# The last of eighteen groups takes the seven-product form of its first matmul; VectorE adds partial sums out of PSUM and scales the group ahead of it

## Chip, core and metric

The kernel runs on one core of a Trainium2 chip. The metric is device time in microseconds (us) of one launch; the time before is the median of nine runs. The engines are TensorE (PE in the profile; PEld is its weight load), VectorE (DVE), ScalarE (ACT), GpSimd (POOL, which here does small arithmetic and starts accumulating DMAs) and SyncE (SP, which starts plain DMAs).

## The reference

The input `x` is (8, 4224, 192) in float32. A causal convolution over the sequence with seven taps comes first, one softmax-normed set of taps for each of eight heads; then a layer norm without an offset, two matmuls with a ReLU between them, and a residual.

```python
w = softmax(weight, axis=-1)                       # (8 heads, 7 taps)
x_unf = x_pad[:, idx, :].reshape(B, S, K, H, group)
x = np.einsum('hk,bskhg->bshg', w, x_unf).reshape(B, S, D)
xn = (x - mu) / np.sqrt(var + 1e-06) * g_ln
ch = np.maximum(xn @ w_ch1, 0.0) @ w_ch2           # 192 -> 768 -> 192
out = x + ch
```

All of it is float32. The kernel folds `g_ln` and the subtraction of the mean into the first weight, so the norm is left as one factor for each row, which is applied to the result of the second matmul (`scale`, with `rstd`).

## The kernel before

**Tiling.** A row of `x` is one position of the sequence. Each of 128 partitions holds a run of neighbouring rows, and a group is up to `J` = 16 rows on every partition. There are 18 groups: three small ones (0 to 2, with 6, 8 and 10 rows), and fifteen of 16 rows (3 to 17). For a group, VectorE and ScalarE compute the convolution into `y`, VectorE transposes it in blocks of 32x32 into `yt` (j rows, `NC` = 6 chunks of 32 channels, 32 columns), TensorE forms the hidden layer (the "up" stage), ScalarE moves it from PSUM into `room` with the ReLU, and TensorE forms the output (the "down" stage). `room` is one buffer; each group uses it anew.

**Matmuls.** In the up stage `rows_of_tiles` issues matmuls of 32 contracted rows; four of them, on four row strips (`NQ` = 4), run together and fill four PSUM banks. One matmul of the program is two MATMUL records of the trace, as float32 goes in two passes. The eight PSUM banks are used as two sets of four (`take_set`).

**Seven products.** Groups in `MIXED` (3 to 16 before) run `up_mixed`. There the `yt` of the group is cut in two by rows and in two by channels (`quarters_of_y`), and the first weight in two by channels and in two by hidden units; two thirds of the hidden units (`PAIR` = 2 of `FC` = 3 chunks in each half) are formed by seven products of quarter size instead of eight (Strassen's scheme in Winograd's form, with sums of quarters made by VectorE in `sums_of_y`), and the remaining chunks by two full products (`plain`). Partial results stay in PSUM from one product to the next (the set called `chain`), and three others are added to a result that already lies in `room`: ScalarE copies the partial sum from PSUM into a spare room (`first`, `second`, `third`), and `close` has GpSimd start a DMA that adds it. Both sets alternate, so a product can begin only when the set's earlier content was read. `up_mixed` also holds, in the order in which they are written, the ScalarE multiplications that scale the output of the group ahead (`scale(g - 1, ...)`), its store (`add_to_out`, a DMA from GpSimd that adds to the output in DRAM) and the next group's taps on VectorE (`conv`).

**Down stage.** `down_fast` forms the output for `fast[g]` rows with seven products again; here VectorE forms the sums (`half_sum`) in `room` itself. For groups 3 to 16 `fast[g]` is all 16 rows. For the last group, 17, `fast` is 11; the other 5 rows go through `down`, plain matmuls, after `down_fast`, so that the end of the kernel has little left after the last matmul.

**The last group before.** Group 17 isn't in `MIXED`. It runs `up`: for each of 6 chunks of hidden units, one product over 11 rows (352 columns) and one over 5 rows (160 columns); ScalarE evicts them, with four instructions for the 11 rows (L519) and one for the 5 (L521). `lower_sum(17)` makes its three sums on VectorE afterwards. Group 16 is scaled by ScalarE between the evictions of the first chunks (16 instructions on L830), and its two stores follow on GpSimd.

The order of instructions on every engine is the order in which the program is written (`manual_schedule`); the framework adds the semaphores.

Of the kernel before, what the change touches and what calls it, by code (L numbers as in the profile page):

```python
# [10 lines left out]
AF = mybir.ActivationFunctionType  # L11
ALU = mybir.AluOpType
# [4 lines left out]
def kernel(  # L17
# [36 lines left out]
    C = 32  # L54
# [25 lines left out]

    MIXED = range(3, NG - 1)
    PAIR = NF // 2 - 1
# [397 lines left out]

    def blocks(g):

        n = groups[g][2]
        cut = fast[g] if 0 < fast[g] < n else n // 2 if n * C > 512 else 0
        return [slice(0, cut), slice(cut, n)] if cut else [slice(0, n)]

    def hidden_tile(g):
        n = groups[g][2]

        cut = NF * NQ * fast[g] * C  # L490
        halves = rest = None
        if fast[g]:
            halves = room[:, 0:cut].rearrange(
                "p (h e f q j t) -> p h e f q j t", h=2, e=2, f=FC, q=NQ, t=width(g)
            )
        if n > fast[g]:
            rest = room[:, cut : NF * NQ * n * C].rearrange(
                "p (f q j t) -> p f q j t", f=NF, q=NQ, t=C
            )
        ht[g] = halves, rest  # L500

    def width(g):

        return T if fast[g] % 2 or fast[g] < groups[g][2] else C

    def evict_up(g, f, js, src):

        halves, rest = ht[g]
        if js.stop > fast[g]:
            dst = rest[:, f, :, js.start - fast[g] : js.stop - fast[g]]  # L510
            src = src.rearrange("p q (j t) -> p q j t", t=C)
        elif width(g) == C:
            dst = halves[:, :, f // FC, f % FC].rearrange("p h q j t -> p q h (j t)")
            src = src.rearrange("p q (h w) -> p q h w", h=2)
        else:
            dst = halves[:, :, f // FC, f % FC, :, js].rearrange("p h q j t -> p q j h t")
            src = src.rearrange("p q (j h t) -> p q j h t", h=2, t=T)
            for q in range(NQ):
                nc.scalar.activation(dst[:, q], src[:, q], AF.Relu)  # L519
            return  # L520
        nc.scalar.activation(dst, src, AF.Relu)  # L521

    def rows_of_tiles(banks, left, right, first=True, last=True):


        chunks, w = right.shape[2] // P, left.shape[1] * C
        for c in range(left.shape[2]):
            for i in range(chunks):
                for q in range(NQ):
                    rows = slice(C * q, C * q + C)  # L530
                    nc.tensor.matmul(  # L531
                        banks[:, q, i * w : i * w + w], right[rows, c, P * i : P * i + P],
                        left[rows, :, c, :], start=(first and c == 0 and i == 0),
                        stop=(last and c == left.shape[2] - 1), skip_group_check=chunks > 1,
                    )

    def up(g):


        scaled = {0: (), 1: (), 2: (0, 1)}.get(g, (g - 1,))  # L540
        hidden_tile(g)
        for f in range(NF):
            for js in blocks(g):
                banks = take_set()
                rows_of_tiles(banks, yt[g][:, js], w1[:, :, f * P : f * P + P])
                evict_up(g, f, js, banks[:, :, 0 : (js.stop - js.start) * C])
            if g == 0 and f < 2:
                first_tap(1, heads=(H // 2 * f, H // 2 * (f + 1)))

            parts = 2 if g + 1 == NG else 4  # L550
            if 1 <= f <= parts:
                for s in scaled:
                    m = groups[s][2]
                    scale(s, m * (f - 1) // parts, m * f // parts)
                    if f % (parts // 2) == 0:
                        add_to_out(s, m * (f - parts // 2) // parts, m * f // parts)

# [15 lines left out]
    def quarters_of_y(g):  # L573
        return [
            yt[g][:, HJ * h : HJ * h + HJ, CH * k : CH * k + CH] for h in range(2) for k in range(2)
        ]

    def sums_of_y(g):

        room = upool.tile([P, 3 * HJ * CH * C], F32, tag="ys", name=f"ysums{g}")  # L580
        room = room.rearrange("p (v j c t) -> p v j c t", v=3, c=CH, t=C)
        ysums[g] = s1, s2, s3 = [room[:, v] for v in range(3)]
# [11 lines left out]
    def up_mixed(g, last_sum):  # L594


        W = HJ * C
        assert groups[g][2] == fast[g] == 2 * HJ and PAIR * W == 512
        hidden_tile(g)
        a = ht[g][0]  # L600
        a11, a12, a21, a22 = quarters_of_y(g)
# [15 lines left out]

        def close(c, part):
            whole = "p f q w -> p (f q w)"
            add_by_dma(c.rearrange(whole), part.rearrange(whole))  # L620

        def plain(f, banks):
            rows_of_tiles(banks, yt[g][:, 0 : 2 * HJ], w1[:, :, f * P : f * P + P])
            evict_up(g, f, slice(0, 2 * HJ), banks)

# [4 lines left out]
        rooms = parts(bpool, "tb"), parts(cpool, "cs")  # L630
        first, second = (r[:, 0:PAIR] for r in rooms)
        rows_of_tiles(chain, a11, b11, True, False)
        evict(chain, c11)
        rows_of_tiles(other, a12, b21)
        evict(other, first)
        close(c11, first)
        rows_of_tiles(chain, s2, w1sums[:, 1], False, False)
        evict(chain, c21)
        scale(g - 1, 0, 1)
        conv(g + 1, 2, 3)  # L640
        next(last_sum)
        rows_of_tiles(other, s3, w1sums[:, 2], True, False)
        evict(other, c22)
        scale(g - 1, 1, 2)
        rows_of_tiles(chain, s1, w1sums[:, 0], False, False)
        evict(chain, second)
        close(c22, second)
        scale(g - 1, 2, 3)
        rows_of_tiles(other, a22, w1sums[:, 3], False)
        for i, room in enumerate(rooms):  # L650
            one, third = slice(i, i + 1), room[:, PAIR : PAIR + 1]
            evict(other, third, i=one)
            close(c21[:, one], third)
        scale(g - 1, 3, 4)
        rows_of_tiles(chain, s2, b22, False)
        evict(chain, c12, True)
        nc.scalar.activation(c11, c11, AF.Relu)
        scale(g - 1, 4, 7)
        conv(g + 1, 3, 6)
        conv(g + 1, 6, K, heads=(0, H // 2))  # L660
        plain(PAIR, other)
        nc.scalar.activation(c22, c22, AF.Relu)
        scale(g - 1, 7, 10)
        add_to_out(g - 1, 0, 8)
        lower_sum(g, (PAIR,))
        lower_sum(g, range(PAIR))
        conv(g + 1, 6, K, heads=(H // 2, H))
        plain(PAIR + FC, chain)
        scale(g - 1, 10, done)
        add_to_out(g - 1, 8, done)  # L670

    po = {}

    def down(g):


        n = groups[g][2]
        t = ht[g][1]
        po[g] = []
        order = [(c, js) for c in range(NC) for js in blocks(g)]  # L680
        if g + 1 == NG:
            order = [(c, slice(fast[g], n)) for c in range(NC)]
        for c, js in order:
            w = (js.stop - js.start) * C
            bank = take_bank()
            for f in range(NF):
                for q in range(NQ):
                    nc.tensor.matmul(  # L688
                        bank[C * q : C * q + C, 0:w], w2[:, f, C * c : C * c + C],
                        t[:, f, q, js.start - fast[g] : js.stop - fast[g], :],  # L690
                        start=(f == 0), stop=(f == NF - 1),
                    )
            po[g].append((c, js, bank[:, 0:w]))
# [7 lines left out]


    def half_sum(g, dst, left, right, op, fs=range(FC)):
        a = ht[g][0]
        for f in fs:
# [4 lines left out]
    def lower_sum(g, fs=range(FC)):  # L710

        a = ht[g][0]
        if g in MIXED:
# [8 lines left out]
    def down_fast(g):  # L722
        n = fast[g]
        t = width(g)
        w = n * T
        a = ht[g][0]
        flat = cpool.tile([P, NC, NFAST * C], F32, tag="cs", name=f"cs{g}")[:, :, 0 : n * C]
# [35 lines left out]

        taps_behind = [0] * 6
        if g in MIXED:
            taps_behind = [1, 4, 4, 7, 0, 0]
        product(0, a[:, 0, 0], b[0], c11, True)
# [6 lines left out]
        some_taps(taps_behind[3])  # L774
        if g in MIXED:
            transpose(g + 1)
            moments(g + 1, 0, EARLY)
# [9 lines left out]
        if g + 1 == NG:  # L787
            finish_fast(g, 0, flat, cs, parts)
        if g in MIXED:
            close_by_dma(c21, parts[0])  # L790
# [7 lines left out]
    def finish_fast(g, half, flat, cs, parts):  # L798
        n = fast[g]
        ot = ots[g] if half else out_tile(g)  # L800
        if half or g not in MIXED:
            fresh = cs[:, CH * half : CH * half + CH, 1]
# [90 lines left out]
    for g in range(NG):  # L893
# [7 lines left out]
        if not fast[g]:  # L901
# [26 lines left out]
            continue  # L928
        if last:
            lower_sum(g)  # L930
        if g + 2 < NG:
# [49 lines left out]
```

## Time and profile before

| | |
|---|---|
| median of nine runs | 977.62 us (975.88 to 978.59) |
| the profiled execution | 977.75 us, its span 976.1 us |
| TensorE busy | 960.9 us, 98% of the span, granted clock 0.998 |
| VectorE busy | 857.0 us, 88% |
| ScalarE busy | 643.3 us, 66% |
| GpSimd busy | 199.1 us, 20% |
| the last three stages of TensorE: up of group 17, its `down_fast`, its `down` | 31.60, 18.93 and 9.78 us |

The span is the time between the first and the last recorded event of the execution; what lies around it is 1.65 us here. Times inside the profile are counted from the span's start. A row of a group of instructions has line, engine, operation, output and inputs, shapes, count, then busy time and the mean of one in ns, then idle time ahead of it and who ended that. The chain that ended last is followed back from the last instruction.

### The profile page before, as it was taken

What the parts mean: (1) busy time and instruction counts of PE and PEld (TensorE: products, weight loads), DVE (VectorE), ACT (ScalarE), POOL (GpSimd) and SP (SyncE); (2) the same over time, 40 slices, a digit from 0 to 9 for tenths busy, and PEclk for the clock granted to TensorE, in tenths of its full rate; (3) what the DMA queues carried; (4) which work ended last, traced back from release to release, by engine and by line L of the source; (5) the groups of instructions that cost most, each with busy time, mean ns of one, the idle gap of its engine ahead of it and who ended that gap; (6) DMA issues with size and microseconds to landing.
All of it is one profiled execution on the core that took longest, in us unless ns stands there. A gap on an engine that the chain in (4) does not pass through costs nothing.

```text
span 976.1 us, 36329 instructions
## 1 busy us (share of the span) xinstructions
PE 960.9 (98%) x16338; PEld 675.9 (69%) x16338; DVE 857.0 (88%) x1479; ACT 643.3 (66%) x1044; POOL 199.1 (20%) x355
## 2 busy tenths in 40 slices
PE   5999999999999999999999999999999999999997
PEld 4886585766768585776858576675857667685787
DVE  5899998898998989899898989899798989989407
ACT  4733757585867858595776858587685858675451
POOL 2004410411114011411114111321104111230200
PEclk9999999999999999999999999999999999999999
DMA  8333689588696968779686978969697887765131
GB/s 185 110 124 132 143 203 255 114 146 257 135 263 126 238 147 162 227 150 271 128 245 126 201 193 151 265 131 252 132 225 169 145 245 139 186 122 94 23 64 67
DMA packets 29962, 163.19 MB, mean 167 GB/s; under 512 B 3567, under 2 KB 9839, under 8 KB 22126
## 3 DMA queue, kind: packets, MB, share of 16 engines
q0 software_dynamic: 22704, 97.53, 53.3%
q1 hardware_dynamic: 6798, 63.34, 17.0%
q8 instruction: 128, 2.10, 0.9%
q14 instruction: 28, 0.23, 0.1%
q10 hardware_dynamic: 304, 0.00, 0.0%
HBM read 38.95 MB, written 50.33 MB: 91 GB/s over the span
## 4 chain that ended last, share of the span: by engine, by line
PE 97%; DMA 2%; DVE 0%; issue 0%; SPq 0%
PE ps L531 49%; PE ps L741 41%; PE ps L688 6%; DMA xg<-in_x_dram 1%; PE ps L320 1%; DMA ga<-in_moe_g_ln_dram 1%; PE ps L332 0%; PE ps L344 0%; PE ps L349 0%; DVE y L844 0%; DVE ot L869 0%; SPq L165 0%; DVE ot L854 0%; DVE y L857 0%
## 5 line engine op out<-in xcount | busy, mean ns | idle before, releaser
L408 DVE SCALAR_TENSOR_TENSOR y<-xg,taps,y 128x384 f32<-128x384 f32 (+3 forms) x734 | 367.9, 576 | 1.8 <-ACT y L383 1.7
L531 PE MATMUL ps<-yt,w 32*128 32x256 f32 (+5 forms) x4128 | 303.5, 446 | 0.0
L531 PEld LDWEIGHTS ps<-yt,w 32*128 32x128 f32 x4128 | 205.1, 185 | 90.5 <-issue 75.0
L741 PE MATMUL ps<-room,w2sums 128*32 128x256 f32 (+1 forms) x4320 | 233.8, 375 | 0.0
L741 PEld LDWEIGHTS ps<-room,w2sums 128*32 128x32 f32 x4320 | 140.4, 110 | 87.9
L706 DVE TENSOR_TENSOR room<-room 128x1024 f32<-128x1024 f32 (+1 forms) x138 | 154.1, 1188 | 35.6 <-ACT part L747 24.2
L741 PE MATMUL ps<-room,w 128*32 128x256 f32 (+1 forms) x3240 | 179.8, 375 | 0.0
L741 PEld LDWEIGHTS ps<-room,w 128*32 128x32 f32 x3240 | 103.8, 110 | 74.3 <-ACT ot L830 10.6
L747 ACT COPY cs<-ps 128x256 f32<-128x256 f32 (+1 forms) x180 | 63.0, 365 | 99.5 <-PE ps L741 98.8
L531 PE MATMUL ps<-ysums,w1sums 32*128 32x256 f32 x2016 | 111.3, 374 | 0.0
L616 ACT COPY room<-ps 128x2048 f32<-128x2048 f32 x42 | 78.4, 1867 | 48.7 <-PE ps L531 47.4
L531 PEld LDWEIGHTS ps<-ysums,w1sums 32*128 32x128 f32 x2016 | 103.7, 185 | 5.1
L805 DVE STREAM_TRANSPOSE ot<-cs 128x512 f32<-128x512 f32 (+1 forms) x90 | 55.9, 672 | 57.5 <-DMA cs<-part 34.4
L521 ACT ACTIVATE room<-ps 128x2048 f32<-128x2048 f32 (+4 forms) x52 | 75.5, 1451 | 35.7 <-PE ps L531 35.6
L830 ACT ACTIVATE ot<-ot,r 128x192 f32<-128x192 f32 x248 | 96.7, 447 | 0.0
L383 ACT ACTIVATE y<-xg,taps 128x384 f32<-128x384 f32 (+3 forms) x141 | 73.3, 590 | 9.3 <-DMA out_dram<-y 6.9
L837 POOL DMA_DIRECT2D out_dram<-ot x40 | 34.2, 1081 | 207.8 <-ACT ot L830 153.0
L439 DVE BATCH_NORM_STATS2 st<-y 128x6 f32<-128x192 f32 x264 | 71.0, 342 | 0.0
L397 POOL DMA_DIRECT2D y<-tb x28 | 24.6, 1037 | 176.2 <-ACT cs L747 172.8
L394 ACT ACTIVATE tb<-xg,taps 128x384 f32<-128x384 f32 x112 | 58.0, 602 | 0.0
L419 DVE STREAM_TRANSPOSE yt<-y 128x3072 f32<-128x3072 f32 (+3 forms) x19 | 56.2, 2958 | 1.9
L688 PE MATMUL ps<-room,w 128*32 128x192 f32 (+3 forms) x1152 | 57.2, 359 | 0.0
(101 smaller groups left out, 758.7 us busy)
## 6 DMA issues: line engine op xcount, KB each, us to landing
xg<-in_x_dram SPq DMA_DIRECT2D x15, 2112.0 KB, 15.1
out_dram<-ot POOLq DMA_DIRECT2D x29, 768.0 KB, 8.0
y<-tb POOLq DMA_DIRECT2D x28, 768.0 KB, 9.2
out_dram<-y SPq DMA_DIRECT2D x13, 1536.0 KB, 10.7
room<-parts_tb POOLq DMA_DIRECT2D x14, 1024.0 KB, 7.4
room<-parts_cs POOLq DMA_DIRECT2D x14, 1024.0 KB, 7.2
room<-parts_tb POOLq DMA_DIRECT2D x14, 512.0 KB, 9.3
room<-parts_cs POOLq DMA_DIRECT2D x14, 512.0 KB, 10.8
```

The lines of the kernel that those rows point to most:

```text
L383: nc.scalar.mul(y[g][:, 0:n, cs], xg[g][:, 0:n, cs], taps[:, h, 0:1])
L394: nc.scalar.mul(tb[g][:, 0:n, cs], xg[g][:, 1 : 1 + n, cs], taps[:, h, 1:2])
L408: nc.vector.scalar_tensor_tensor(out=y[g][:, 0:n, cs], in0=t[:, k : k + n, cs], scalar=taps[:, h, k : k + 1], in1=y[g][:, 0:n, cs], op0=AL ...
L439: nc.vector.bn_stats(out=sums[g][:, j, :], in_=y[g][:, j, :])
L521: nc.scalar.activation(dst, src, AF.Relu)
L531: nc.tensor.matmul(banks[:, q, i * w : i * w + w], right[rows, c, P * i : P * i + P], left[rows, :, c, :], start=(first and c == 0 and i = ...
L616: nc.scalar.activation(dst, src, AF.Relu) if relu else nc.scalar.copy(dst, src)
L688: nc.tensor.matmul(bank[C * q : C * q + C, 0:w], w2[:, f, C * c : C * c + C], t[:, f, q, js.start - fast[g] : js.stop - fast[g], :], start ...
L706: nc.vector.tensor_tensor(a[:, *dst, f], a[:, *left, f], a[:, *right, f], op=op)
L741: nc.tensor.matmul(dst[C * q : C * q + C, 0:w], right[:, f, C * c : C * c + C], left[:, f, q], start=(first and f == 0), stop=(f == FC - 1 ...
L747: nc.scalar.copy(to[:, c], dst[:, 0:w].rearrange("p (j t) -> p j t", t=t))
L830: nc.scalar.mul(ots[g][:, j, :], ots[g][:, j, :], rstd[g][:, j : j + 1])
```

## The change

Group 17 joins `MIXED` and runs `up_mixed`, then `down_fast` and `down` as before. Five things follow from this.

- Its 16 rows all take part in the seven products. Because `down_fast` of this group works on 11 of the 16 rows, the half-and-half cut isn't made between rows: `quarters_of_y` cuts each block of 32 columns into two of `T` = 16. `room` has one layout for all 16 rows (`h e f q j t`, t = 16), and `of_products` is the view of the first 11.
- In this group, `close` is one VectorE addition that reads the partial sum in PSUM and adds it into `room`, with no copy by ScalarE and no DMA.
- The scaling of group 16 is done by two VectorE multiplications over 8 rows each, put behind the second product's sum; its two stores follow them.
- `sums_of_y(17)` is made by VectorE in the down stage of group 16, ahead of `finish_fast(16)`, as for other groups. `lower_sum` is the form with the ReLU in it, and covers 11 rows; the 5 others of that quarter get their ReLU from ScalarE (`rest`).
- `down(17)` reads its 5 rows out of the new layout, in runs of 16 elements.

Helpers lose arguments that only the old form of the last group needed (`blocks`, the row slices of `evict_up`). The instructions of groups 0 to 15 stay what they were.

```diff
-    MIXED = range(3, NG - 1)
+    MIXED = range(3, NG)
...
     def quarters_of_y(g):
-        return [
-            yt[g][:, HJ * h : HJ * h + HJ, CH * k : CH * k + CH] for h in range(2) for k in range(2)
-        ]
+        if width(g) == C:
+            cuts = [(slice(HJ * h, HJ * h + HJ), slice(0, C)) for h in range(2)]
+        else:
+            cuts = [(slice(0, J), slice(T * h, T * h + T)) for h in range(2)]
+        return [yt[g][:, js, CH * k : CH * k + CH, ts] for js, ts in cuts for k in range(2)]
...
-        def close(c, part):
+        def close(c, banks, part, i=slice(0, PAIR)):
+            if last:
+                src = banks.rearrange("p q (f w) -> p f q w", w=W)[:, i]
+                nc.vector.tensor_tensor(c[:, i], c[:, i], src, op=ALU.add)
+                return
+            evict(banks, part, i=i)
             whole = "p f q w -> p (f q w)"
-            add_by_dma(c.rearrange(whole), part.rearrange(whole))
+            add_by_dma(c[:, i].rearrange(whole), part.rearrange(whole))
...
         rows_of_tiles(other, a12, b21)
-        evict(other, first)
-        close(c11, first)
+        close(c11, other, first)
         rows_of_tiles(chain, s2, w1sums[:, 1], False, False)
         evict(chain, c21)
-        scale(g - 1, 0, 1)
-        conv(g + 1, 2, 3)
+        act_scales(0, 1)
+        taps_of_next(2, 3)
         next(last_sum)
+        if last:
+            for j1 in (0, HJ):
+                part, factor = ots[g - 1][:, j1 : j1 + HJ], rstd[g - 1][:, j1 : j1 + HJ]
+                nc.vector.tensor_tensor(
+                    part, part, factor.unsqueeze(2).to_broadcast([P, HJ, D]), op=ALU.mult
+                )
+                add_to_out(g - 1, j1, j1 + HJ)
...
         plain(PAIR + FC, chain)
-        scale(g - 1, 10, done)
-        add_to_out(g - 1, 8, done)
+        if last:
+            rest = a[:, 1, 0, 0:PAIR, :, fast[g] :]
+            for f in range(PAIR):
+                nc.scalar.activation(rest[:, f], rest[:, f], AF.Relu)
+        else:
+            scale(g - 1, 10, done)
+            add_to_out(g - 1, 8, done)
...
+    def of_products(g):
+        return ht[g][:, :, :, :, :, 0 : fast[g] * T // width(g), :]
...
     def down(g):
+                    if fast[g]:
+                        left = ht[g][:, :, f // FC, f % FC, q, js].rearrange("p h j t -> p j h t")
...
-        if last:
-            lower_sum(g)
```

## The prediction

> **What bounds the kernel now.** I read the page's chain first, then the chain in order of time for the last two groups, then ScalarE's and VectorE's timelines over the same stretch, and last the groups by shape, for durations.
>
> ```profile
> PE 97%; DMA 2%; DVE 0%; issue 0%; SPq 0%
> ```
>
> The page's chain: 97% of the span is TensorE. So only TensorE's own time, waits put into it, and the few us behind the last matmul can move the result.
>
> ```profile
> 23.52 1.72 PE ps L320 x14
> ...
> 854.69 28.64 PE ps L531 x432
> 883.34 27.33 PE ps L741 x504
> 910.67 31.60 PE ps L531 x553
> 942.27 18.93 PE ps L741 x504
> 961.20 8.20 PE ps L688 x240
> 969.42 0.36 DVE ot L869
> ```
>
> The chain in order of time: start, us, engine, output, line, records. The up stage of group 16 (L531, from 854.69) takes 28.64 us in 432 records, that of group 17 (from 910.67) 31.60 us (576 records, some missing). The stages follow one another to the hundredth: nothing stalls TensorE. The last 8.20 us of L688 are cut off by the chain; the stage lasts 9.78 us by TensorE's busy time in that window.
>
> ```profile
> 860.20 1.87 ACT L616 COPY parts_tb<-ps 128x2048 f32<-128x2048 f32 x1 [0.77 <-PE ps L531]
> 862.74 1.87 ACT L616 COPY room<-ps 128x2048 f32<-128x2048 f32 x1 [0.68 <-PE ps L531]
> ...
> 865.33 1.87 ACT L616 COPY room<-ps 128x2048 f32<-128x2048 f32 x1 [0.37 <-PE ps L531]
> ```
>
> ScalarE in group 16: the evictions of the second, third and fourth product. Each waits for TensorE, takes 1.87 us, and the next product ends 2.59 us later: 0.7 us of slack for whoever reads a PSUM set.
>
> ```profile
> 905.82 1.65 DVE L439 BATCH_NORM_STATS2 st<-y 128x6 f32<-128x192 f32 x6
> 908.47 1.90 DVE L805 STREAM_TRANSPOSE ot<-cs 128x512 f32<-128x512 f32 x3 [0.99 <-DVE st L439]
> 910.29 0.92 DVE L803 TENSOR_TENSOR cs<-cs,room 128x768 f32<-128x768 f32 x1
> 911.31 1.90 DVE L805 STREAM_TRANSPOSE ot<-cs 128x512 f32<-128x512 f32 x3
> ```
>
> VectorE around the start of group 17's up stage: it is done with group 16 at 913.2, and in that stage it is almost empty (three sums of 0.89 us).
>
> ```profile
> L706 DVE TENSOR_TENSOR room<-room 128x1024 f32<-128x1024 f32 x126 | 144.1, 1217 | 1.5 <-ACT part L747 1.5
> L782 DVE TENSOR_TENSOR cs<-cs,ps 128x256 f32<-128x256 f32 x42 | 15.0, 412 | 0.0
> L586 DVE TENSOR_TENSOR ysums<-yt 128x768 f32<-128x768 f32 x14 | 13.9, 991 | 0.0
> L706 DVE TENSOR_TENSOR room<-room 128x704 f32<-128x704 f32 x12 | 10.0, 887 | 34.1 <-ACT part L747 22.7 <-ACT room L519 11.5
> ```
>
> VectorE's additions by shape, behind the bar the busy us and the mean of one in ns: the prices for the new ones.
>
> **The change, part by part.**
>
> *TensorE's columns.* Before, group 17 streams 6 chunks x 6 channel chunks x 4 strips x 512 columns. Now it is seven products of 24 matmuls x 256 columns and two of 24 x 512: 67584 columns instead of 73728. That is exactly group 16's stage, so I take its row: 28.64 us. By columns alone 31.60 would become 28.97; the other 0.33 is what the cut into 352 and 160 columns costs (28.64 us for 67584 columns gives 31.24 for 73728, not 31.60). Removed: 31.60 − 28.64 = 2.96 us, all on the path.
>
> *Runs of 16.* The products of group 17 read `yt` in runs of 16 floats, where group 16 reads runs of 32; `down(17)` reads its 5 rows in runs of 16 as well. No row has runs of 16. The nearest is L320, with runs of 24: 14 records of 144 columns in 1.72 us, 0.853 ns a column, against 28.64 us / 33792 (four strips at once, two records each) = 0.848 in group 16. The difference, if it is the runs', is 0.13 ns a run; 16 runs in 256 columns give 2 ns on 217, or 1%. On 18.2 us of products and 9.8 us of `down` that is 0.28 us. I take 0 (0.848 is the same for runs of 32 and for longer contiguous ones), and keep 0.28 as the cost's near end. [...]
>
> *VectorE closes from PSUM.* Four additions: two of 2048 elements (`c11`, `c22`), two of 1024 (`c21`). From 704 and 1024 elements (887 and 1217 ns) the slope is 1.031 ns an element; the row with a PSUM operand, 256 elements in 412 ns, lies at the line's 425, so PSUM adds nothing. 2048 elements: 1217 + 1024 x 1.031 = 2.27 us; two of 1024 back to back: 1.14 (the step of nine in 10.29 us) + 1.22 = 2.36 us. TensorE waits for these at three places: the fourth product needs the set that `c11`'s close reads, the seventh the one of `c22`'s, the first plain product the one of `c21`'s two. Each has one product of 2.60 us for it. ScalarE's copies begin 0.07 to 0.30 us behind the end of the matmuls as the chain has it; I give VectorE the same 0.30, and 0.05 for the way back (L245's last result at 14.55, TensorE's L329 at 14.60). That is 2.62, 2.62 and 2.71 against 2.60: stalls of 0.02, 0.02 and 0.11, with the short wait (0.07) none at all. I take 0.2 in all for a matmul pipeline that restarts; ends 0 and 1.0 (0.3 at each place). [...]
>
> *Is VectorE free when the second product ends?* That is at 910.67 + 5.21 = 915.88. `sums_of_y(17)` puts three additions (0.94, 0.96, 0.99 as L586; 2.85 us with overlap) ahead of the transposes at 908.47. These now start at 907.47 + 2.85 = 910.3, as the 0.99 us of waiting fill up, and VectorE is free at 915.1: 0.8 us to spare. The sums themselves are first needed by the third product at 915.9 and are ready at 910.3. Behind the first close wait: the fourth sum (0.95, needed by the seventh product, 7 us later), two scalings of 1536 elements (1217 + 512 x 1.031 = 1.75 each), then `c22`'s close. 918.5 + 0.2 + 0.95 + 3.5 = 923.1, against the fifth product's end at 923.7. Nothing on TensorE waits for the three `lower_sum` operations (0.89 each) before the second down product at about 942. Cost: 0, with 0.6 us to spare; without that cover, a late close stalls TensorE by as much as it is late.
>
> *Scaling of group 16.* 16 ScalarE instructions leave (5.7 us busy, beside TensorE: worth nothing), two VectorE ones come, above. The two stores of 768 KB move from 925.32 and 930.50 to about 921.4 and 923.1; GpSimd has nothing else in its queue there, and they land some 7.4 us later, 40 us before the end. Cost 0.
>
> *ScalarE.* Four evictions and two ReLUs of 1.9 us, two evictions in four parts for the plain chunks (512 elements a part, 0.52 us a step from L519's and L521's rows, so 2.07) and two small ReLUs (`rest`, about 0.5 each) are some 16.5 us in a stage of 28.8. At its end ScalarE is done about 3.1 us after TensorE. The first down product takes 2.70 us and needs none of that but the first of the four parts (0.6 us); the third needs the plain chunk, 5.4 us after; `rest` is read by `down(17)`, 19 us after. Cost 0; if the second product waited for `rest`, which lies between its rows, 0.4.
>
> *Down stages and tail.* `down_fast(17)` keeps 504 records of 176 columns and the same nine sums (704 elements, in four runs of 176): 18.93. `down(17)`: 9.78. Behind it the same transposes and store. They all move earlier by what the up stage gains.
>
> *Sum.* 2.96 − 0.2 = 2.76 us. On the profiled execution's own time, 977.75 (span 976.1 and 1.65 around it): 974.99. That execution lies 0.13 above the median, so I forecast 974.9 for the median, 0.28% less. A measurement of this kernel can tell about 0.2%, 1.95 us, from no change.
>
> **The rivals.**
>
> *A: waits take most of the gain.* VectorE's close is on a cycle of 2.6 us with next to no slack, where ScalarE had 0.7. For: the sum above is within 0.1 us of the limit at three places. Against: VectorE is otherwise idle, and PSUM costs it nothing in L782. At 0.3 to 0.6 us each, with the 0.28 of the runs, the gain falls to 1.8 or 0.9: 975.8 to 976.7, no change that can be told.
>
> *B, on the other side: runs of 16 slow TensorE's stream.* Place: the seven products (18.2 us) and `down(17)` (9.8 us), 28.0 us together. It decides from 2.76 / 28.0 = 9.9% on, that is 21 ns for a matmul record of 256 columns, or 1.3 ns for each run. At three columns lost a run (2.5 ns, 18.8%) the cost is 5.3 us: 980.1, slower by 2.5. For: no row has such runs. Against: runs of 24 bound it at a tenth of that price.
>
> *C: it does not do what it says.* The group may wait for something that leaves it no better than before: VectorE falling behind group 16 (its transposes wait for a DMA at 908.47) delays the first close. Each us it is later than 915.9 is a us lost; for the gain to be gone the transposes would have to start at 913.9 instead of 910.3, the DMA to land 5.4 us later than it did: 977.6. The same DMA made VectorE wait 4.4 us in group 15, where second taps' DMAs share the queues; group 16 has none.
>
> **How the numbers follow.** The forecast has 0.76, A 0.11, B 0.09, C 0.04. Of the forecast a small part falls within 0.2%, since runs of one kernel spread from 975.88 to 978.59. That gives faster 0.73, same 0.16, slower 0.11. The range: at the low end no stall (974.7 on the median) and 1.2 us of the spread downward, 973.5; at the high end A's 976.7. That leaves out B, C's worst and some of the spread, about 2 in 10.
>
> **What would show it.** Right: group 17's up stage at 28.6 to 29.0 us with 432 records on L531, `down_fast` 18.9 and `down` 9.8 unchanged, VectorE's closes from PSUM at about 2.27 and 1.2 us beginning within 0.3 us of a product's end, the first at about 916.2. A would show as gaps on TensorE ended by DVE `room` at the fourth, seventh and eighth product; B as an L531 stage above 30 us and L688 above 10 us with no gaps; C as a gap ahead of the fourth product and a first close long after 916.2. I am wrong if group 17's stage takes over 29.6 us, or if anything in the stages behind it grows.

## The result, and the profile after

| | before | after |
|---|---|---|
| median | 977.48 us (30 runs, 975.79 to 978.66) | 973.11 us (10 runs, 972.58 to 975.01) |
| profiled execution, its span | 977.75, 976.1 us | 972.58, 970.9 us |
| up stage of group 17 | 31.60 us | 28.99 us |
| `down_fast`, `down` of group 17 | 18.93, 9.78 us | 18.93, 9.78 us |

The changed kernel is faster: the ratio is 0.9961, with a 95% interval of 0.9954 to 0.9969. That is 4.4 us by the medians, where 2.7 were forecast; the median lies 0.4 us under the low end of the range. The stage that the change touches gained 2.61 us. In the two profiles the rest lies in the first 32 us, ahead of everything that the change touches.

The chain in order of time, after (start, us, engine, output, line, records):

```profile
880.76 27.33 PE ps L762 x504
908.09 28.99 PE ps L521 x432
937.08 18.93 PE ps L762 x504
956.01 8.19 PE ps L707 x240
964.23 0.36 DVE ot L888
```

Group 17's up stage (L521 now) has the 432 records of the other mixed groups and takes 0.35 us more than their 28.64. Behind it everything is as long as before, and TensorE is still the chain.

VectorE's timeline in that stage, after:

```profile
910.38 1.90 DVE L824 STREAM_TRANSPOSE ot<-cs 128x512 f32<-128x512 f32 x3
913.62 2.29 DVE L614 TENSOR_TENSOR room<-room,ps 128x2048 f32<-128x2048 f32 x1 [1.34 <-PE ps L521]
916.14 0.96 DVE L578 TENSOR_TENSOR ysums<-yt,ysums 128x768 f32<-128x768 f32 x1 [0.23 <-PE ps L521]
917.01 3.42 DVE L652 TENSOR_TENSOR ot<-ot,r 128x1536 f32<-128x1536 f32 x2
921.56 2.29 DVE L614 TENSOR_TENSOR room<-room,ps 128x2048 f32<-128x2048 f32 x1 [1.13 <-PE ps L521]
924.08 2.35 DVE L614 TENSOR_TENSOR room<-room,ps 128x1024 f32<-128x1024 f32 x2 [0.23 <-PE ps L521]
```

VectorE is done with group 16 at 912.28, 1.0 us ahead of the second product's end (908.09 + 5.21 = 913.30). The closes take 2.29 and 2.35 us and begin 0.2 to 0.3 us behind a product. TensorE's weight loads show what that costs:

```profile
915.96 5.06 PEld L521 LDWEIGHTS ps<-ysums,w1sums 32*128 32x128 f32 x96 [0.29 <-DVE room L614]
923.90 2.47 PEld L521 LDWEIGHTS ps<-ysums,w 32*128 32x128 f32 x48 [0.29 <-DVE room L614]
```

The weight loads of the fourth and of the seventh product wait for the close (L614) that reads their set; the first close ends at 915.91, the load starts at 915.96. TensorE's timeline in the same stage, then the same rows of group 16 in this profile:

```profile
913.30 8.12 PE L521 MATMUL ps<-ysums,w1sums 32*128 32x256 f32 x144
921.25 2.77 PE L521 MATMUL ps<-yt,w1sums 32*128 32x256 f32 x48
...
926.60 10.48 PE L521 MATMUL ps<-yt,w 32*128 32x512 f32 x96
```

```profile
857.33 7.95 PE L521 MATMUL ps<-ysums,w1sums 32*128 32x256 f32 x144
865.10 2.77 PE L521 MATMUL ps<-yt,w1sums 32*128 32x256 f32 x48
...
870.28 10.48 PE L521 MATMUL ps<-yt,w 32*128 32x512 f32 x96
```

From start to start, the third to fifth product take 7.95 us (913.30 to 921.25) where group 16's take 7.77, and the sixth and seventh 5.35 (921.25 to 926.60) where group 16's take 5.18: 0.18 and 0.17 us, together the 0.35 that group 17 has over group 16.

The rest of the profiles' difference is in the first 32 us. Rows of the chain, and one row each from the table of stretches (20 to 22 us: busy us by engine, then the granted clock, DMA share, GB/s), first of before, then of after:

```profile
18.59 2.49 PE ps L320 x14
21.08 2.44 PE ps L332 x4
20.00:22.00 2.00, 2.00 (x7) 1.54 (x7) 2.00 (x8) 0.46 (x2) 0.00 (x0) 0.50 0.80 151
```

```profile
17.55 1.95 PE ps L320 x14
19.50 1.29 PE ps L332 x4
20.00:22.00 2.00, 2.00 (x15) 1.74 (x14) 2.00 (x9) 0.96 (x2) 0.00 (x0) 1.00 0.93 167
```

The same instructions ran at half the clock before, and `x` had landed 1.0 us later, so that group 0's first product began 2.73 us later (31.47 against 28.74). From the end of group 0's up stage to the end of the span it is 976.1 − 44.59 = 931.51 against 970.9 − 41.86 = 929.04. Whether this start belongs to the change was the first thing to test.

### The profile page after: what moved, and what is told of

It is laid out like the page before. It is cut to its first block, busy times and chain, and to the rows that moved or that the text cites. A ratio compares the mean times of both kernels' runs of the same rounds, so it can differ in the third digit from the quotient of the medians.

```text
span 970.9 us, 36017 instructions
## 1 busy us (share of the span) xinstructions
PE 956.8 (99%) x16194; PEld 669.1 (69%) x16194; DVE 870.6 (90%) x1489; ACT 640.3 (66%) x1014; POOL 201.1 (21%) x355
## 4 chain that ended last, share of the span: by engine, by line
PE 98%; DMA 2%; DVE 0%; issue 0%; SPq 0%
PE ps L521 49%; PE ps L762 41%; PE ps L707 6%; DMA xg<-in_x_dram 1%; PE ps L320 1%; DMA ga<-in_moe_g_ln_dram 1%; PE ps L344 0%; PE ps L349 0%; DVE y L863 0%; PE ps L332 0%; DVE ot L888 0%; SPq L165 0%; DVE ot L873 0%; DVE y L876 0%
## 5 line engine op out<-in xcount | busy, mean ns | idle before, releaser
L521 PE MATMUL ps<-yt,w 32*128 32x256 f32 (+3 forms) x3744 | 287.7, 458 | 0.0
L521 PEld LDWEIGHTS ps<-yt,w 32*128 32x128 f32 x3744 | 187.9, 185 | 91.1 <-issue 81.0
L727 DVE TENSOR_TENSOR room<-room 128x1024 f32<-128x1024 f32 (+1 forms) x135 | 151.4, 1194 | 9.6 <-ACT part L768 9.6
L607 ACT COPY room<-ps 128x2048 f32<-128x2048 f32 x45 | 84.0, 1867 | 55.4 <-PE ps L521 52.7
L521 PE MATMUL ps<-ysums,w1sums 32*128 32x256 f32 x2160 | 119.4, 374 | 0.0
L521 PEld LDWEIGHTS ps<-ysums,w1sums 32*128 32x128 f32 x2160 | 110.6, 185 | 6.1 <-DVE room L614 0.3
L511 ACT ACTIVATE room<-ps 128x2048 f32<-128x2048 f32 (+3 forms) x46 | 71.2, 1548 | 33.6 <-PE ps L521 33.6
L849 ACT ACTIVATE ot<-ot,r 128x192 f32<-128x192 f32 x232 | 90.9, 447 | 0.0
L736 DVE SCALAR_TENSOR_TENSOR room<-room 128x1024 f32<-128x1024 f32 (+1 forms) x45 | 51.4, 1194 | 8.8 <-ACT room L509 7.6
```

What stands on the lines that cost most here:

```text
L521: nc.tensor.matmul(banks[:, q, i * w : i * w + w], right[rows, c, P * i : P * i + P], left[rows, :, c, :], start=(first and c == 0 and i = ...
L607: nc.scalar.activation(dst, src, AF.Relu) if relu else nc.scalar.copy(dst, src)
L727: nc.vector.tensor_tensor(a[:, *dst, f], a[:, *left, f], a[:, *right, f], op=op)
L849: nc.scalar.mul(ots[g][:, j, :], ots[g][:, j, :], rstd[g][:, j : j + 1])
```

## The experiments

**Is the excess the start's?** Theory S says that TensorE's clock at the start is drawn anew in every execution; rival E that the change gains outside the last group. The changed kernel was run again, and both kernels with 16 more idle matmuls at the start (all idle matmuls share one PSUM bank, so the others take turns as before):

```diff
-    keep_warm(20)
+    keep_warm(30)
...
             nc.tensor.matmul(pm[r], share[0], w1f[:, r, :], start=True, stop=False)
+        keep_warm(6)
         conv_on_pe(PE_HEADS[0])
```

> The changed kernel once more, unedited. Theory S (the last group's up stage is worth 2.6 us, and whatever goes beyond that is the state of the start: TensorE's clock and the landing of x in the first 24 us, which differ from execution to execution): single times in two clusters about 1.7 us apart, near 972.8 and 974.5, and up stage of group 17 at 28.99 us again. Rival E (the change is worth 4 us and more through something outside the last group): the stages of groups 0 to 16 differ from those of the kernel before, and the times do not fall back.

Measured: median 973.97 (six runs: 973.05 to 973.45, and 974.49 to 974.59), ratio 0.9959 (0.9947 to 0.997). Up stage 28.99 again. Its profile caught a cold start: the granted clock was 0.50 between 18 and 20 us, L320's 14 records took 3.70 us, and its span is 1.9 us longer than the one above, with the same rows behind group 0. The fall back that S expects is there.

> The kernel before with 16 more idle matmuls at the start: 10 behind the 20 that are there, 6 between the first matmuls of the weight's centring and the first convolution on TensorE, so that TensorE does not stand idle for 2.4 us twice before x lands. S: the clock of 0.50 between 20 and 22 us does not come back, the two matmuls pairs of L332 take 1.3 us instead of 2.4, the upper cluster (977.3 to 978.7) disappears, median about 976.0 with a spread under 1.2 us: 1.5 us less than the kernel before. E or no effect of the clock: median 977.5, spread as before.

Measured: 976.35 (975.48 to 977.15), 1.5 us under the kernel before beside it (977.83). The clock is 1.00 in every stretch from 16 to 28 us, L332's counterpart takes 1.29 us. The upper cluster is gone; the spread of 1.7 us is more than expected.

> The changed kernel with the same 16 idle matmuls. S: its median lies 2.6 us (2.3 to 2.9) below that of the warm kernel before, about 973.3 or less, and its upper cluster (974.2 to 975.0) is gone. E: it lies 4 us or more below the warm kernel before.

Measured: 973.36 (972.84 to 973.60). The pair differs by 2.99 us, slightly over what S gave. Hence a second pair, loaded anew:

> The warm kernel before once more, loaded anew and beside its counterpart, to see whether the excess of the first pair (976.35 against 973.36, 2.99 us, where the traces behind group 0 differ by 2.6 to 2.7) is the landing of x, drawn anew in each execution. Draw: median 976.0 to 976.5. Systematic rival: 976.3 or more again, and x landing later in its profile than in the warm changed kernel's again (18.5 against 17.6 us).

> The warm changed kernel once more. Draw: the difference of the two medians between 2.4 and 3.0 us, so about 973.5, and the landing of x in the profile anywhere from 17.4 to 18.6 us. Systematic rival: 3.0 us or more below the warm kernel before again, 973.3 or less, and x at 17.4 to 17.8 us.

Measured: 976.29 and 973.06, apart by 3.23 us; L320 began at 18.09 and 17.93. From the end of group 0's up stage to the end of the span, the three profiles with the old last group that these pairs and the first page give have 931.51, 931.42 and 931.69 us, the four with the new one 929.04, 928.82, 928.76 and 928.85: 2.67 apart in the mean. Up to the start of group 17's up stage all seven take 866.02 to 866.28 us, so the groups in between gained nothing. E falls: behind the start, the change is worth 2.6 to 2.7 us, all of it in the last group.

The clock explains a part of the excess. Of the 62 runs of the kernel before in the three comparisons with the most of them, 40 lie in the upper cluster (over 977); of 16 of the changed one, 6 do (over 974). Of the 41 runs of the kernel before that were made beside the experiments, all 12 with a mean clock of 0.999 or more lie in the lower cluster and all 20 with 0.997 or less in the upper one; the 9 with 0.998 lie in both. In the first comparison 18 of 30 runs before and 3 of 10 after are in the upper cluster, so one median lies in each. Cluster against cluster (medians 976.10 and 972.89, 977.76 and 974.57) that comparison gives 3.2 us instead of 4.4; the second, with the changed kernel's six new runs, gives 3.4 and 3.65 instead of 3.9.

So 0.3 to 1.0 us over the traces' 2.67 stay, 0.32 and 0.56 of it in the warm pairs, where the clock is 1.00 in all four profiles. Later landing of `x` would be: L320 began at 18.59, 18.67 and 18.09 us in the profiles of the kernel before and at 17.55 to 17.99 in all ten with the new last group. But in `uncut_before`, below, which also has the old form, it began at 17.61. Whether the change moves the landing of `x`, and by what, stays open.

The five kernels that were run once (this next one, the three behind it, and the late stores) are judged by their stages, as the start alone moves a run by some 1.7 us (the medians of the two clusters above, 976.10 and 977.76).

**The removed term: is 0.33 us the price of the cut?** In the kernel before, one product over all 16 rows, and only the evictions cut:

```diff
-            for js in blocks(g):
-                banks = take_set()
-                rows_of_tiles(banks, yt[g][:, js], w1[:, :, f * P : f * P + P])
-                evict_up(g, f, js, banks[:, :, 0 : (js.stop - js.start) * C])
+            banks = take_set()
+            rows_of_tiles(banks, yt[g][:, 0 : groups[g][2]], w1[:, :, f * P : f * P + P])
+            for js in blocks(g):
+                evict_up(g, f, js, banks[:, :, js.start * C : js.stop * C])
```

> The kernel before, but the last group's up stage streams all 16 rows in one product of 512 columns and only the evictions are cut into 11 and 5 rows: 288 records instead of 576. If the price of the cut into 352 and 160 columns is 0.33 us, as the prediction's first step has it, the up stage of group 17 goes from 31.60 to 31.24 us (73728 columns at group 16's rate). Rival: the 0.33 us is no price of the cut (a wait, or the rate of runs), and the stage stays at 31.6.

The chain in order of time:

```profile
910.26 31.11 PE ps L531 x288
941.37 0.83 PE ps L741 x17
942.20 0.71 ACT room L519 x2
942.92 0.61 ACT room L521
943.57 17.21 PE ps L741 x456
```

The stage takes 31.11 us: the cut cost 0.49. But nothing is gained. The eviction of the last chunk's 11 rows now starts as the stage ends (941.38), where it started 1.9 us ahead of the end before (940.35, end at 942.27); `down_fast` waits for ScalarE, and from the stage's start to `down`'s it is 50.52 us against 50.53 before.

**What does a late close cost?** The two scalings and their stores moved ahead of the second product and its close:

> The changed kernel with the two scalings of group 16 (3.42 us on VectorE) and their stores ahead of the first close instead of behind it. Theory: a close has no slack, so TensorE loses each us that VectorE is late, one for one. VectorE is free at 912.3 on the changed kernel's scale, scales until 915.65, and the first close begins 2.0 us later than the 913.62 of the changed kernel: up stage of group 17 at 31.0 us instead of 28.99, all of it at the fourth product; down stages unchanged. Rival (the closes have slack that the model of ends hides): 29.0 to 29.5 us.

VectorE's first close, and TensorE's row behind the gap:

```profile
916.41 2.28 DVE L614 TENSOR_TENSOR room<-room,ps 128x2048 f32<-128x2048 f32 x1
918.74 5.46 PE L521 MATMUL ps<-ysums,w1sums 32*128 32x256 f32 x96 [2.24 <-DVE room L614]
```

The stage runs from 908.44 to 939.78: 31.34 us, 2.35 more than the changed kernel's. A close on time would have begun at 914.0; it was 2.4 late. One for one, as the theory has it (it said 31.0, since I had VectorE free 0.3 us earlier). With the scalings there, the change would keep 0.26 us of its gain.

**Does it matter who scales group 16?** All 16 rows on ScalarE, as in groups 3 to 15 (`scale` without `if not last`), closes unchanged:

> The changed kernel with group 16 scaled by 16 ScalarE instructions in the same places as in groups 3 to 15, the closes by VectorE kept. Theory: where the scaling is done is worth nothing in the up stage (28.99 us). At its end six scalings and the ReLU of the five rows stand ahead of the copies of the first down products: ScalarE gets to them 2.2 us later than in the changed kernel, the copy that the third down product needs ends at about +6.0 us of that stage against its start at +5.4: down_fast 18.93 + 0.6 = 19.5 us. Rival: no difference in either stage (28.99 and 18.93).

```profile
939.46 2.05 ACT ot L838 x6
...
943.09 2.89 PE L751 MATMUL ps<-room,w2sums 128*32 128x176 f32 x72 [0.21 <-ACT cs L757]
```

The first row is from the chain, the second from TensorE's timeline. The up stage took 29.02 us; up and `down_fast` together 956.73 − 908.39 = 48.34, which leaves 19.32 for the second: 0.39 us lost to six scalings ahead of the copies. The forecast had the 16 instructions' removal as worth nothing; it is worth 0.4 us where the shorter down products of this group begin.

**Is adding out of PSUM needed?** The VectorE branch of `close` removed, so ScalarE copies and a DMA adds:

> The changed kernel with the last group's closes as in groups 3 to 16: ScalarE copies the partial sum, GpSimd's DMA adds it. Scaling stays on VectorE. Theory: the two gaps of 0.17 us go, as ScalarE's copy of 1.87 us leaves 0.4 us of slack: up stage 28.64 us. The DMAs for c21 begin at about +17.5 and land by +28, the three sums of lower_sum are done by +30.5, the second down product needs them at +31.3: down_fast stays at 18.93, so the kernel is 0.35 us faster than the changed one. Rival: the DMAs land too late in this shorter stage, and the second down product waits 0.5 to 2 us for lower_sum; then adding out of PSUM is what made the form usable in the last group.

From the list of waits around the start of `down_fast`:

```profile
DVE room L732 <- DMA room<-parts_tb: 4.6, 1, 4.6
PE ps L758 <- DVE room L732: 1.9, 1, 1.9
```

My theory missed and the rival held. The up stage is 28.64 us, free of gaps. But c21's partial sums landed 13.3 and 15.3 us after their issue, `lower_sum` (L732) waited for them, and TensorE waited 0.45 us for ScalarE and 1.89 for `lower_sum`. Up and `down_fast` together take 50.45 us (908.25 to 958.70), where the kernel before has 50.53: the whole gain is gone.

Why so late? The two stores of group 16 were issued at 919 and 921, and the DMA engines were full from 918 to 938 (a share of 0.94 to 1.07 in each 4 us, 0.61 in the next). So, the same kernel with `add_to_out` behind c21's closes:

> As close_by_dma, but group 16's two stores of 768 KB are started behind the closes of c21 instead of ahead of c22's. Theory: in close_by_dma the stores (at 919 and 921) lay ahead of the closes in the DMA engines, which were full from 918 to 940, so c21 landed 13 and 15 us after its start instead of 9 and 11 as in group 16; with the stores behind, c21 lands by about +29 of the up stage, up 28.64, and the second down product waits 0 to 0.7 us instead of 1.9 and 0.45. Rival: the closes themselves fill the DMA engines (or the stores still share them), and the wait stays at 1.5 us or more.

DMA issues (name, queue, count, KB, us to landing), first of the kernel with the early stores, then of this one; then this one's chain:

```profile
room<-parts_tb POOLq DMA_DIRECT2D x1, 512.0 KB, 13.3
room<-parts_cs POOLq DMA_DIRECT2D x1, 512.0 KB, 15.3
```

```profile
room<-parts_tb POOLq DMA_DIRECT2D x1, 512.0 KB, 8.0
room<-parts_cs POOLq DMA_DIRECT2D x1, 512.0 KB, 10.3
```

```profile
910.46 28.64 PE ps L521 x432
939.11 18.93 PE ps L760 x504
```

The partial sums land 5 us sooner and neither stage has a gap: the two together take 0.35 us less than in the changed kernel (its one run, 974.72 us, caught a cold start, L320's 14 records in 3.70 us). It was the order of DMAs, not the way of adding. VectorE's addition starts no such DMA, so in the changed kernel the early stores have nothing to hold up.

**Can the two gaps go with closes by VectorE?** First, VectorE adds one of the two chunks of c11 and c22 and ScalarE copies the other for a DMA (with the idle matmuls of the warm kernels):

```diff
+            if last and i.stop - i.start == 2:
+                half = slice(0, 1)
+                src = banks.rearrange("p q (f w) -> p f q w", w=W)[:, half]
+                nc.vector.tensor_tensor(c[:, half], c[:, half], src, op=ALU.add)
+                i, part = slice(1, 2), part[:, 1:2]
```

> The changed kernel with the 16 idle matmuls at the start, and with the closes of c11 and c22 split: VectorE adds one of their two chunks out of PSUM (1024 elements, 1.2 us), ScalarE copies the other (1.0 us) and a DMA adds it, so that the PSUM set is free after 1.5 us instead of 2.6. Theory: both gaps go, up stage of group 17 at 28.64 us, down_fast at 18.93, and 0.35 us less than the warm changed kernel's 973.36: 973.0 (972.5 to 973.4), 3.4 us less than the warm kernel before. Rival: the DMA parts land late and the ReLUs of c11 and c22 hold up ScalarE's evictions, 28.9 us or more.

```profile
915.47 1.01 ACT L612 COPY parts_tb<-ps 128x1024 f32<-128x1024 f32 x1 [2.05 <-DVE room L620]
```

A miss: 28.96 us. Both halves lie in the same four banks, and the copy began as the addition ended (914.22 + 1.22 = 915.44); the two together are as long as the whole (914.22 to 916.48 is 2.26 us, against 2.29). The median of 972.87 (972.74 to 973.24) is therefore no gain of the split. Then cut between banks, two for each engine:

> As split_close_warm, but the closes of c11 and c22 are cut between PSUM banks: VectorE adds out of two of a set's four banks, ScalarE copies the other two and two DMAs add them. In split_close_warm both read the same four banks, ScalarE began only when VectorE had ended, and the gaps stayed. Theory: now both read at once, the set is free 1.3 us after the product, both gaps go: up stage 28.64 us, down_fast 18.93, 0.35 us below the warm changed kernel. Rival: ScalarE still waits for VectorE, 28.95 us.

```profile
914.04 1.01 ACT L621 COPY parts_tb<-ps 128x1024 f32<-128x1024 f32 x1 [0.75 <-PE ps L526]
926.78 0.31 PEld L526 LDWEIGHTS ps<-yt,w 32*128 32x128 f32 x8 [0.28 <-DVE room L628]
```

Now both read at once (VectorE's addition begins at 914.06), and both gaps are gone; but the stage is 28.81 us, as the seventh product, on time at last, exposes a gap of 0.17 at the third place, c21's two closes. The median is 972.77 (972.45 to 973.27), ratio 0.9953 (0.9939 to 0.9967): with the start kept warm, the lowest of the medians here, though its runs overlap with those of the split before it and of the warm changed kernel. The late stores together with the warm start weren't run.

## Why the prediction was right or wrong

*Removed columns.* Right: 432 records, and 28.64 us for them where nothing waits (late stores). The split of the 2.96 us was off: 0.49 of it is the cut, not 0.33.

*Runs of 16.* Right, and rival B with its 0.28 us falls: the first two products, in runs of 16, take 5.21 us, as 2 x 2.60 in group 16, and `down` 9.78 as before.

*Closes.* The durations were right (2.29 for 2.27, 2.35 for 2.36), and so was the wait on the set as the only new one. A PSUM source cost VectorE nothing that shows, as taken: 1024 elements took 1.22 us out of PSUM (both split kernels) and 1.217 out of SBUF (L706). The stalls were mis-sized and misplaced: I took 0.2 us in all with 0.11 at c21, and measured 0.18 at the fourth product, 0.17 at the seventh and none at c21. The way back was 0.05 as taken. The first close began 0.32 us behind its product, which with 2.29 and 0.05 makes 2.66 against 2.60: 0.06 us late where I had 0.02. The other 0.12 us I put down to the restart, for which I had no row and which I booked once and not for each place; no run shows such a restart, only the two gaps, and what the 0.12 consists of is not shown. (Weight loads that don't wait begin 0.2 us ahead of their product, 913.09 against 913.30; behind the late close of `scale_first` load and product both begin at 918.74.) c21's gap exists only if the seventh product is on time.

*Cover by VectorE.* Right: 1.0 us to spare where I had 0.8, and a late close cost what it was late (rival C's price, shown with the scalings first: 2.4 us late, 2.35 lost).

*ScalarE.* Right that its work ends behind TensorE without harm (939.87, 2.8 us after; I had 3.1). "Worth nothing" for the removed scalings was wrong by 0.4 us.

*The sum.* 2.76 forecast, 2.61 in the stage: the mechanism was right, and the stalls are the term that was too small (0.35 for 0.2). The step that failed is the last one, from the profiled execution to the median: it took for granted that the changed kernel's runs would have the same starts as those of the kernel before. The range allowed 1.2 us for the runs' spread around the median; but the two clusters lie some 1.7 apart (976.10 and 977.76), and 18 of 30 runs lay in the upper cluster before and 3 of 10 after, which makes 1.2 of the 1.7 us by which the medians' 4.4 exceeds the 2.67 of the traces. The other 0.5 has no shown cause. No run shows a reason for the unequal shares (10 of 17 and 3 of 6 in the second comparison); so few runs can differ like that by chance. Rival A didn't happen: 0.35 us is an eighth of the gain.

## What to carry to other kernels

Before a small change is costed, look at whether single runs fall into clusters, and find the cluster in the trace: where two profiles differ ahead of the changed stage, compare them stage by stage and not by their spans. Where two PSUM sets alternate as here, whoever reads a set has one product's time for it (2.60 us), the waits included: a close of 2.29 us that began 0.32 behind its product cost 0.18, and one that was 2.4 late cost 2.35. And a partial sum that goes by DMA landed later for what was issued ahead of it (13.3 and 15.3 us behind two stores, 8.0 and 10.3 ahead of them), so stores that nobody waits for belong behind it.

## What was not expected of the hardware

TensorE's granted clock fell to 0.50 behind idle stretches of 2.75 to 3.35 us. In the profiles without the extra idle matmuls, TensorE stands idle ahead of L329's four matmuls. In the changed kernel's first profile that stretch lasted 2.29 us, and the clock stayed at 1.00. In the kernel before (2.75 us), in `uncut_before` (2.88) and in the changed kernel's second profile (3.35) the clock fell to 0.50: between 20 and 22 us in the first of these, between 18 and 20 us in the other two, where L329's four matmuls already took 1.85 and 2.58 us instead of 1.56. So what looks drawn anew in each run goes, in these four, with the length of this stretch, which differs between executions of the same instructions (2.29 and 3.35 us in two of the changed kernel). Four profiles don't make a threshold, and the second stretch, ahead of L320 (2.43 us), may have its share where the first lasted 2.75 us. In all six profiles with sixteen more idle matmuls the clock was 1.00 from 16 to 24 us, and the kernel before took 1.5 us less with them (976.35 against 977.83).

An accumulating DMA of 512 KB within SBUF landed after 8.0 and 10.3 us with group 16's stores issued behind it, and after 13.3 and 15.3 us with the stores ahead of it. ScalarE and VectorE read different banks of a PSUM set at once (both began at 914.04 to 914.06 us).
